# Pooled attention and two dense blocks on one core: VectorE takes over GpSimd's float additions

## The chip, the cores and the metric

One core of one Trainium2 chip runs the whole program. The metric is the device time of one execution in microseconds (us); the figure of a kernel is the median of several executions, and beside it stands one execution that the hardware profiler recorded. The engines are called TensorE (PE, matrix products; PEld is its loading of weights), VectorE (DVE), ScalarE (ACT), GpSimd (POOL) and SyncE (SP, the queue from which all transfers are issued). Each engine works off its own instructions in the order in which they were built.

## The reference

```python
# attention: q, k, v are [8, 8, 576, 64]
k_p = k.reshape(B, H, Sp, 8, D).mean(axis=3)      # Sp = 72
v_p = v.reshape(B, H, Sp, 8, D).mean(axis=3)
scores = (q @ k_p.T) / sqrt(D)
x = softmax(scores) @ v_p                          # -> [4608, 512]
# block 1, weights 512x2048 and 2048x512
h = x @ w_in;  g = where(h >= 1, h, where(h <= -1, 0, (h + 1)**2 / 4))
x2 = g @ w_out
# block 2
h = x2 @ w_in2; r = maximum(h, 0); out = (r * r) @ w_out2
```

The weights arrive as 64-bit words of two 32-bit halves; the kernel makes one float of each pair (`convert_w`). A product in full precision is made of three fast ones, from a rounded part and a remainder of each factor (hi and lo): hi x hi, lo x hi, hi x lo.

## The kernel before

**Order of the program.** The program is written as a list of steps; a scheduler then orders the instructions of each engine when the program is built, by their place in the program and by when it expects their inputs, and inserts the waits. An engine that it expects to be free takes later work that is ready, so pooling runs well ahead of its place in the text. At run time each engine keeps the order given.

**Stages.** The start (about 0 to 45 us) does the attention of the first block of 512 tokens. Then come steps `s`, sixteen (`f`) for each block of 512 tokens: `gemm1` (L656, L666) multiplies x by one column block of the first weights into `ph`; `step_ops` (L670) makes `u` (ScalarE, L689/L690), `g` (VectorE, L699), `gh` (ScalarE, L701) and `gl` (VectorE, L707); `gemm2` (L719, L738) adds `g` times the second weights to four accumulators, two steps later (`LAG`). For each step ScalarE makes `wihi` and `wohi` (L217) and VectorE their remainders `wilo` and `wolo` (L221), from the weights in SBUF. The attention of the next tokens is cut into units that stand between the matmuls (`slots`, L514). From step 28 in the program's text the second block's weights are prepared (`prepare_w2`, L176), and from about 900 us on block 2 runs: its first 512 tokens in the same steps, the rest with seven products in place of eight (L1003, L1012), whose weights are sums and differences of quarters of the weight matrices.

**Weights of block 2.** For each of 16 pairs of weight tiles `prepare_w2` loads both, converts them (`convert_w`, L134: ScalarE, three VectorE operations at L153, L156, L159, one integer addition on GpSimd at L162), forms four sums of quarters (`s1` to `s4`, L196 to L199) and stores all eight quarters as hi and lo with `keep_w2` (L169): ScalarE rounds (L172), an engine given as `lo_on` subtracts (L173), SP stores (L174). Four `keep_w2` calls belong to a pair: VectorE subtracts in two of them and GpSimd in the other two.

**Pooling.** `load_kv` (L267) brings 8 x 64 numbers of 72 groups and two heads as a tile `kv` of 72x2x512; three such buffers exist, and a load waits for the work on the tile that held the buffer. `pool_kv` (L278) halves it by additions: 512, 256, then 128 elements on 72 partitions. Batch 0 has the first two halvings on VectorE for keys and on GpSimd for values (L284), and TensorE does the rest; batches 1 and 2 are pooled by TensorE; batches 3 to 7 (40 tiles) are pooled by GpSimd alone (L297 twice, L298 once). The results `kp` and `vp` go to TensorE's transposes and products.

## Time and profile before

| | |
|---|---|
| median of three runs | 1673.24 us (1672.28 to 1678.28) |
| the profiled execution: its time, its span | 1679.75 us, 1677.7 us |
| TensorE busy (share of the span) | 1640.4 us (98%) |
| VectorE busy | 1237.9 us (74%) |
| ScalarE busy | 885.0 us (53%) |
| GpSimd busy | 327.6 us (20%) |
| mean granted clock of TensorE | 0.989 |

The span runs from the first to the last instruction, the execution's own time is 2.05 us longer. Shares of busy time are averages over stages of different kinds, so the profile is read by stages. A busy TensorE isn't TensorE at its peak: matmuls overlap, and their ends are modelled. Durations of one instruction are in ns in the groups and in us in the timeline; a bracket at the end of a row of the timeline says how long the engine was idle before it and what ended that.

### The profile page before, as it was taken

What the parts mean: (1) busy time and instruction counts of PE and PEld (TensorE: products, weight loads), DVE (VectorE), ACT (ScalarE), POOL (GpSimd) and SP (SyncE); (2) the same over time, 40 slices, a digit from 0 to 9 for tenths busy, and PEclk for the clock granted to TensorE, in tenths of its full rate; (3) what the DMA queues carried; (4) which work ended last, traced back from release to release, by engine and by line L of the source; (5) the groups of instructions that cost most, each with busy time, mean ns of one, the idle gap of its engine ahead of it and who ended that gap; (6) DMA issues with size and microseconds to landing.
All of it is one profiled execution on the core that took longest, in us unless ns stands there. A gap on an engine that the chain in (4) does not pass through costs nothing.

```text
span 1677.7 us, 23589 instructions
## 1 busy us (share of the span) xinstructions
PE 1640.4 (98%) x7952; PEld 1322.4 (79%) x7952; DVE 1237.9 (74%) x1973; ACT 885.0 (53%) x1603; POOL 327.6 (20%) x299
## 2 busy tenths in 40 slices
PE   7899999999999899999999999999999999999998
PEld 6665788888887687878888888888888878887886
DVE  5998578888888888888886452569557856885585
ACT  5655455656566465766666542346435533553353
POOL 3444144542435515231230000000000000000000
PEclk7999999999999999999999999999999999999999
DMA  9475535435354445443543085567686777677675
GB/s 240 134 217 152 144 83 155 148 108 161 112 158 141 118 122 181 123 132 103 192 170 128 7 295 176 170 193 231 191 255 218 207 204 238 213 207 227 194 206 135
DMA packets 276728, 284.72 MB, mean 170 GB/s; under 512 B 151168, under 2 KB 179840, under 8 KB 276608
## 3 DMA queue, kind: packets, MB, share of 16 engines
q1 hardware_dynamic: 276608, 283.21, 56.4%
q8 instruction: 64, 1.05, 0.3%
q14 instruction: 56, 0.46, 0.1%
HBM read 218.10 MB, written 65.01 MB: 169 GB/s over the span
## 4 chain that ended last, share of the span: by engine, by line
PE 84%; DVE 8%; DMA 3%; issue 2%; ACT 1%; POOL 1%; SPq 1%; DVEq 0%; POOLq 0%; ACTq 0%
PE ph L666 22%; PE acc L738 20%; PE dp L1012 10%; PE cp L1003 10%; PE dq L1012 5%; PE cr L1003 5%; PE cq L1003 3%; PE dr L1012 3%; PE px L488 2%; PE pss L372 2%; PE acc L727 2%; DVE wilo L221 1%; DMA w<-w2i 1%; DVE wolo L221 1%; DMA st<-in_moe_w_out_dram 1%
## 5 line engine op out<-in xcount | busy, mean ns | idle before, releaser
L666 PE MATMUL ph<-xhi,wihi 128*128 128x512 f32 x576 | 233.4, 406 | 6.8 <-DVE g L699 5.7
L666 PE MATMUL ph<-xlo,wihi 128*128 128x512 f32 x576 | 226.4, 393 | 0.0
L666 PE MATMUL ph<-xhi,wilo 128*128 128x512 f32 x576 | 226.2, 393 | 0.0
L960 ACT ACTIVATE gh<-g 128x512 fp32r<-128x512 f32 x224 | 139.7, 630 | 151.7 <-DVE g L1029 48.0
L738 PE MATMUL acc<-gh,wohi 128*128 128x512 f32 x512 | 205.9, 402 | 0.0
L738 PE MATMUL acc<-gh,wolo 128*128 128x512 f32 x512 | 200.1, 391 | 1.5 <-DVE wolo L221 1.5
L738 PE MATMUL acc<-gl,wohi 128*128 128x512 f32 x512 | 200.2, 391 | 0.0
L1003 PE MATMUL cp<-x,w 128*128 128x512 f32 x768 | 187.0, 390 | 1.0 <-DMA w<-w2i 0.7
L768 DVE TENSOR_TENSOR gl<-g,gh 128x512 fp32r<-128x512 f32 x224 | 151.3, 687 | 47.6 <-ACT gh L960 46.2
L1003 PEld LDWEIGHTS cp<-x,w 128*128 128x128 f32 x768 | 143.5, 188 | 33.6 <-issue 2.2
L221 DVE TENSOR_TENSOR wilo<-wi,wihi 128x512 fp32r<-128x512 f32 x144 | 123.4, 857 | 58.3 <-ACT wihi L217 57.3
L1012 PE MATMUL dp<-gh,w 128*128 128x512 f32 x512 | 161.5, 389 | 0.0
L707 DVE TENSOR_TENSOR gl<-g,gh 128x512 fp32r<-128x512 f32 x144 | 114.3, 794 | 56.7 <-ACT gh L701 54.1
L666 PEld LDWEIGHTS ph<-xhi,wihi 128*128 128x128 f32 x576 | 109.2, 190 | 35.2 <-DVE g L699 6.1
L217 ACT ACTIVATE wihi<-wi 128x512 fp32r<-128x512 f32 x144 | 89.8, 624 | 81.2 <-PE ph L666 81.0
L666 PEld LDWEIGHTS ph<-xhi,wilo 128*128 128x128 f32 x576 | 109.3, 190 | 23.5
L666 PEld LDWEIGHTS ph<-xlo,wihi 128*128 128x128 f32 x576 | 109.3, 190 | 22.4 <-issue 1.0
L701 ACT ACTIVATE gh<-g 128x512 fp32r<-128x512 f32 x128 | 80.3, 628 | 84.1 <-DVE g L699 83.5
L297 POOL TENSOR_TENSOR kv<-kv 72x512 f32<-72x512 f32 x80 | 93.7, 1173 | 158.4 <-DMA kv<-in_k_dram 81.6
L221 DVE TENSOR_TENSOR wolo<-wo,wohi 128x512 fp32r<-128x512 f32 x128 | 109.2, 853 | 15.3 <-ACT wohi L217 15.1
L1025 ACT ACTIVATE s<-cp 128x512 f32<-128x512 f32 x96 | 57.2, 595 | 118.7 <-PE cp L1003 118.7
L738 PEld LDWEIGHTS acc<-gh,wolo 128*128 128x128 f32 x512 | 96.3, 188 | 21.4 <-DVE wolo L221 2.9
(144 smaller groups left out, 3208.7 us busy)
## 6 DMA issues: line engine op xcount, KB each, us to landing
w<-w2i SPq DMA_DIRECT2D x224, 256.0 KB
w<-w2o SPq DMA_DIRECT2D x224, 256.0 KB
w2i<-cb SPq DMA_DIRECT2D x32, 512.0 KB
w2o<-cb SPq DMA_DIRECT2D x32, 512.0 KB
st<-in_moe_w_out_dram SPq DMA_DIRECT2D x31, 512.0 KB
st<-in_moe_w_in_dram SPq DMA_DIRECT2D x29, 512.0 KB
pd<-pad SPq DMA_DIRECT2D x32, 384.0 KB
z<-pd SPq DMA_DIRECT2D x96, 128.0 KB
```

The source lines that it names most:

```text
L217: nc.scalar.activation(out=hi, in_=src, func=AF.Copy)
L221: eng.tensor_tensor(out=lo, in0=src, in1=hi.bitcast(F32), op=ALU.subtract)
L297: nc.gpsimd.tensor_tensor(out=a[:, :, 0:w], in0=a[:, :, 0:w], in1=a[:, :, w:2 * w], op=ALU.add)
L666: nc.tensor.matmul(out=ph, lhsT=a[:, kk % a.shape[1], :], rhs=c[:, kk, :], start=(i == 0), stop=(i == 3 * KD - 1))
L701: act(out=gh, in_=g, func=AF.Copy)
L707: nc.vector.tensor_tensor(out=gl, in0=g, in1=gh.bitcast(F32), op=ALU.subtract)
L738: nc.tensor.matmul(out=o, lhsT=lhsT, rhs=rhs, start=(f == 0 and x == 0), stop=(f == KF - 1 and x == 2),)
L768: tt(out=out, in0=a, in1=b, op=ALU.subtract)
L960: act(out=hi, in_=a, func=AF.Copy)
L1003: nc.tensor.matmul(out=out[0], lhsT=w[:, a, k, :], rhs=xq[b, i][c][:, k, :], start=(n == 0 and i in (1, 2, 7)), stop=(n == 5), skip_group_ ...
L1012: nc.tensor.matmul(out=out[d], lhsT=w[:, a, d, :], rhs=x[c], start=(g == 0 and n == 0 and i in (1, 2, 7, 4)), stop=(g == NG - 1 and n == 2 ...
L1025: act(out=snaps[key], in_=a, func=AF.Copy)
```

## The change

Every floating-point operation of GpSimd goes to VectorE: the value tiles of batch 0 (8 additions), the pooling of batches 3 to 7 (120 additions), the four sums of quarters of each of 16 pairs (64), and the remainders of these sums (32). GpSimd keeps the 64 integer additions of L162 and some fills of constants.

```diff
-    def keep_w2(kind, g, n, two, lo_on):
+    def keep_w2(kind, g, n, two):
...
-        lo_on.tensor_tensor(out=c[:, :, 1, :], in0=two, in1=c[:, :, 0, :].bitcast(F32), op=ALU.subtract)
+        nc.vector.tensor_tensor(out=c[:, :, 1, :], in0=two, in1=c[:, :, 0, :].bitcast(F32), op=ALU.subtract)
...
-            keep_w2(kind, g, 2 * i, two[i], nc.vector)
+            keep_w2(kind, g, 2 * i, two[i])
...
-        nc.gpsimd.tensor_tensor(out=s1, in0=a21, in1=a22, op=ALU.add)
-        nc.gpsimd.tensor_tensor(out=s2, in0=s1, in1=a11, op=ALU.subtract)
-        nc.gpsimd.tensor_tensor(out=s3, in0=a11, in1=a21, op=ALU.subtract)
-        nc.gpsimd.tensor_tensor(out=s4, in0=a12, in1=s2, op=ALU.subtract)
+        nc.vector.tensor_tensor(out=s1, in0=a21, in1=a22, op=ALU.add)
+        nc.vector.tensor_tensor(out=s2, in0=s1, in1=a11, op=ALU.subtract)
+        nc.vector.tensor_tensor(out=s3, in0=a11, in1=a21, op=ALU.subtract)
+        nc.vector.tensor_tensor(out=s4, in0=a12, in1=s2, op=ALU.subtract)
         yield
-        keep_w2(kind, g, 4, s12, nc.gpsimd)
+        keep_w2(kind, g, 4, s12)
         yield
-        keep_w2(kind, g, 6, s34, nc.gpsimd)
+        keep_w2(kind, g, 6, s34)
...
-                (nc.vector if nm == "k" else nc.gpsimd).tensor_tensor(
-                    out=a[:, :, 0:w], in0=a[:, :, 0:w], in1=a[:, :, w:2 * w], op=ALU.add
-                )
+                nc.vector.tensor_tensor(out=a[:, :, 0:w], in0=a[:, :, 0:w], in1=a[:, :, w:2 * w], op=ALU.add)
...
-            nc.gpsimd.tensor_tensor(out=a[:, :, 0:w], in0=a[:, :, 0:w], in1=a[:, :, w:2 * w], op=ALU.add)
-        nc.gpsimd.tensor_tensor(out=o, in0=a[:, :, 0:D], in1=a[:, :, D:2 * D], op=ALU.add)
+            nc.vector.tensor_tensor(out=a[:, :, 0:w], in0=a[:, :, 0:w], in1=a[:, :, w:2 * w], op=ALU.add)
+        nc.vector.tensor_tensor(out=o, in0=a[:, :, 0:D], in1=a[:, :, D:2 * D], op=ALU.add)
```

The scheduler makes a new order from this. Two places of it follow; lines after L284 are lower by two in the changed kernel. First GpSimd, before, at the first pair of weights of block 2 and the first pooling of batch 3 (`z` is a converted tile, `s` a pair of sums, `cb` a tile to be stored):

```order
L162 TENSOR_TENSOR z<-st,z 128x512 x2
L196 TENSOR_TENSOR s_2712<-z 128x256
L197 TENSOR_TENSOR s_2712<-s_2712,z 128x256
L198 TENSOR_TENSOR z<-z 128x256
L199 TENSOR_TENSOR z<-z,s_2712 128x256
L173 TENSOR_TENSOR cb<-s_2712,cb 128x2x256
L173 TENSOR_TENSOR cb<-z,cb 128x2x256
L162 TENSOR_TENSOR z<-st,z 128x512
L297 TENSOR_TENSOR kv<-kv 72x2x256
L297 TENSOR_TENSOR kv<-kv 72x2x128
L298 TENSOR_TENSOR kp<-kv 72x128
```

GpSimd in the changed kernel, from the last conversions of block 1 to its end:

```order
L162 TENSOR_TENSOR wo_1275<-low_1277,wo_1275 128x512
L162 TENSOR_TENSOR wi_1279<-low_1281,wi_1279 128x512
L162 TENSOR_TENSOR wo_1341<-low_1343,wo_1341 128x512
L162 TENSOR_TENSOR wo_1345<-low_1347,wo_1345 128x512
L162 TENSOR_TENSOR wo_1407<-low_1409,wo_1407 128x512
L162 TENSOR_TENSOR wo_1411<-low_1413,wo_1411 128x512
L162 TENSOR_TENSOR z<-st,z 128x512 x32
```

The integer additions for block 2 now follow each other with nothing between them. The other place is VectorE's order where the first keys of batch 3 are pooled, before (`pn` and `mx` belong to the softmax, `aT` is a turned tile of probabilities):

```order
L699 SCALAR_TENSOR_TENSOR g<-ph,u 128x512
L707 TENSOR_TENSOR gl<-g,gh 128x512
L221 TENSOR_TENSOR wolo<-wo_720,wohi 128x512
L478 STREAM_TRANSPOSE aT<-z 96x1024
L221 TENSOR_TENSOR wilo<-wi_657,wihi 128x512
L390 TENSOR_REDUCE mx<-pss 128x4
L699 SCALAR_TENSOR_TENSOR g<-ph,u 128x512
```

and in the changed kernel:

```order
L697 SCALAR_TENSOR_TENSOR g<-ph,u 128x512
L295 TENSOR_TENSOR kv<-kv 72x2x256
L295 TENSOR_TENSOR kv<-kv 72x2x128
L705 TENSOR_TENSOR gl<-g,gh 128x512
L221 TENSOR_TENSOR wolo<-wo_720,wohi 128x512
L476 STREAM_TRANSPOSE aT<-z 96x1024
L296 TENSOR_TENSOR kp<-kv 72x128
L221 TENSOR_TENSOR wilo<-wi_657,wihi 128x512
L388 TENSOR_REDUCE mx<-pss 128x4
L697 SCALAR_TENSOR_TENSOR g<-ph,u 128x512
```

The three additions of a key tile stand between the operations of a step, the first of them right behind `g` and ahead of `gl`.

## Rows read from the trace of the kernel before

**Rows 1.** Busy time by stages; each engine's us and (instructions), clock, DMA share, GB/s.
```profile
50.00:150.00 100.00, 91.90 (x526) 60.12 (x524) 94.83 (x156) 60.72 (x113) 41.91 (x29) 1.00 0.65 186
150.00:900.00 750.00, 741.13 (x3835) 598.37 (x3835) 611.72 (x974) 454.52 (x842) 269.81 (x248) 1.00 0.46 142
900.00:1050.00 150.00, 150.00 (x664) 124.20 (x663) 70.58 (x108) 65.84 (x112) 0.00 (x0) 1.00 0.41 134
```
**Rows 2.** Busy time in three short stretches (PE, PEld, DVE, ACT, POOL, clock).
```profile
570.00:590.00 20.00, 13.09 (x46) 10.09 (x45) 17.84 (x22) 8.83 (x16) 10.69 (x10) 0.83 0.38 107
650.00:675.00 25.00, 24.19 (x121) 19.63 (x120) 21.38 (x34) 13.35 (x25) 11.44 (x10) 1.00 0.49 163
800.00:825.00 25.00, 24.18 (x121) 19.80 (x120) 20.84 (x39) 14.80 (x27) 2.96 (x2) 1.00 0.44 147
```
**Rows 3.** Timeline from 570 us: start, duration, engine, operation, idle time before and releaser.
```profile
570.43 2.69 DVE L221 TENSOR_TENSOR wolo<-wo,wohi 128x512 fp32r<-128x512 f32 x1
...
572.54 4.64 POOL L297 TENSOR_TENSOR kv<-kv 72x512 f32<-72x512 f32 x4
...
573.18 0.50 PE L738 MATMUL acc<-gh,wolo 128*128 128x512 f32 x1 [1.20 <-DVE wolo L221]
...
576.52 2.42 DVE L221 TENSOR_TENSOR wilo<-wi,wihi 128x512 fp32r<-128x512 f32 x1
...
578.87 2.14 DVE L441 TENSOR_TENSOR pad<-pn,sm 128x256 f32<-128x256 f32 x2
...
581.67 0.80 PE L666 MATMUL ph<-xhi,wihi 128*128 128x512 f32 x1 [5.71 <-DVE g L699]
```
**Rows 4.** Chain that ended last, after that stop: start, us, what.
```profile
581.67 5.49 PE ph L666 x12
...
590.68 2.72 PE ph L666 x12
```
**Rows 5.** Groups of VectorE between 900 and 1050 us, GpSimd idle (busy us, mean ns).
```profile
L707 DVE TENSOR_TENSOR gl<-g,gh 128x512 fp32r<-128x512 f32 x28 | 19.4, 692 | 10.7 <-ACT gh L701 9.1
...
L221 DVE TENSOR_TENSOR wolo<-wo,wohi 128x512 fp32r<-128x512 f32 x13 | 8.9, 686 | 0.0
```
**Rows 6.** Groups of VectorE between 150 and 900 us.
```profile
L221 DVE TENSOR_TENSOR wilo<-wi,wihi 128x512 fp32r<-128x512 f32 x118 | 101.9, 864 | 40.4 <-ACT wihi L217 40.3
L221 DVE TENSOR_TENSOR wolo<-wo,wohi 128x512 fp32r<-128x512 f32 x113 | 97.8, 865 | 13.2 <-ACT wohi L217 13.0
L707 DVE TENSOR_TENSOR gl<-g,gh 128x512 fp32r<-128x512 f32 x115 | 94.2, 820 | 45.8 <-ACT gh L701 45.1
L699 DVE SCALAR_TENSOR_TENSOR g<-ph,u 128x512 f32<-128x512 f32 x115 | 78.3, 681 | 7.9 <-ACT u L690 7.4
L441 DVE TENSOR_TENSOR pad<-pn,sm 128x256 f32<-128x256 f32 x56 | 37.5, 689 | 0.3
```
**Rows 7.** Groups of VectorE over the span: pooling of keys in the start.
```profile
L284 DVE TENSOR_TENSOR kv<-kv 72x512 f32<-72x512 f32 x4 | 2.7, 687 | 6.7 <-DMA kv<-in_k_dram 6.7
...
L284 DVE TENSOR_TENSOR kv<-kv 72x256 f32<-72x256 f32 x4 | 1.7, 420 | 0.1
```
**Rows 8.** Groups of GpSimd over the span: the integer additions for block 2.
```profile
L162 POOL TENSOR_TENSOR z<-st,z 128x512 int32<-128x512 int32 x32 | 50.3, 1573 | 302.6 <-DVE z L159 102.0 <-ACT wohi L217 58.7 <-ACT u L689 45.7
```
**Rows 9.** Timeline of VectorE in the start.
```profile
19.80 0.95 DVE L432 TENSOR_SCALAR sm<-sm 128x8 f32<-128x8 f32 x1
...
24.98 1.23 DVE L432 TENSOR_SCALAR sm<-sm 128x8 f32<-128x8 f32 x1
...
27.58 0.16 DVE L432 TENSOR_SCALAR sm<-sm 128x8 f32<-128x8 f32 x1
...
37.05 0.69 DVE L221 TENSOR_TENSOR wilo<-wi,wihi 128x512 fp32r<-128x512 f32 x1 [4.23 <-ACT wihi L217]
```
**Rows 10.** Waits of GpSimd: us in total, times, longest.
```profile
POOL kv L297 <- DMA kv<-in_k_dram: 81.6, 10, 12.8
POOL kv L297 <- DMA kv<-in_v_dram: 73.7, 7, 14.4
```

## The prediction

> **What bounds the kernel now.** I first read the busy table of the stages [rows 1]. From 150 to 900 us TensorE is busy for 741.13 of 750 us at full granted clock, and in this stretch lie all of the weight sums and of the pooling for batches 3 to 7. VectorE is busy for 611.72 us there (82%), GpSimd for 269.81 us. From 50 to 150 us it is the other way round: VectorE has 94.83 of 100 us, TensorE only 91.90; GpSimd does nothing there but integer additions (29 of them), which the change keeps. From 900 us GpSimd's column is empty. So time can be won only where TensorE stands still between 150 and 900 us, or in the start.
>
> The busy table of three short stretches [rows 2] and the timeline around 570 us [rows 3] show such places. At 570.43 VectorE's remainder `wolo` takes 2.69 us and at 576.52 `wilo` takes 2.42 us, two `pad` products behind them 2.14 us, while GpSimd runs without a pause through pooling and remainders (four additions from 572.54 in 4.64 us). TensorE waits 1.20 us for `wolo`, then 5.71 us for `g`, which stood behind all this in VectorE's queue. The stop costs twice: the granted clock of 570 to 590 us falls to 0.83, and the twelve matmuls of the next step take 5.49 us, those of the step after 2.72 us [rows 4].
>
> Why VectorE is slow there is read from one operation in two stages. With GpSimd idle a remainder of 128x512 takes 0.69 us [rows 5]; between 150 and 900 us the same ones take 0.864, 0.865 and 0.820 us on the mean [rows 6]. The `g` of L699, one input of which is in PSUM, takes 0.681 us in this stretch, as long as any without GpSimd beside it. So it is GpSimd running at the same time that stretches what reads two operands from SBUF.
>
> **The change part by part.** *Added to VectorE after 150 us.* Pooling: 40 pairs of additions on 72x512 and 72x256 elements. On VectorE these shapes stand in the start, with 0.687 and 0.420 us [rows 7]; 40 x 1.107 = 44.3 us. The 40 last additions on 72x128 are not in VectorE's trace; they lie between 0.16 us (a scalar operation on 8 elements, [rows 9]) and 0.420 us (256 elements). I take 0.29 us, since 128 elements lie about halfway: 11.6 us (6.4 to 16.8). The Trainium skill, "VectorE: DVE Perf Modes", section "Side-by-side: where the cycles go for N=2048 bf16", would price this addition at about 0.30 us (128 + 8 + 150 cycles at 0.96 GHz); my estimate from it is 11.9 us, no different sum. Weight sums: 64 on 128x256 at 0.420 us = 26.9 us; remainders: 32 on 128x512 at 0.687 us = 22.0 us. Together 104.8 us (99.6 to 110).
>
> *Taken from VectorE.* What GpSimd costs it now after 150 us: `wilo` 118 x (0.864 - 0.686), `wolo` 113 x (0.865 - 0.686), `gl` 115 x (0.820 - 0.692), `pad` 56 x (0.689 - 0.420) us [rows 5 to 7] = 21.0 + 20.2 + 14.7 + 15.1 = 71 us; smaller groups I leave out. The 31 integer additions that start after 150 us (the first of the 32 for block 2 starts just before) hold 31 x 1.573 = 48.8 of GpSimd's 269.81 us [rows 1, 8], or 18%; I let 82% of the loss go, 58 us (bounds: nothing, or all 71 us). So VectorE gets 104.8 - 58 = 47 us more: 659 of 750 us, 88% (85% to 96%). That isn't full, and TensorE remains the bound of the stretch; on the path this costs 0.
>
> The bounds take in a rule. The Trainium skill, "SBUF — State Buffer", section "Who interferes with whom", says that a VectorE instruction with two SBUF inputs and a GpSimd instruction that reads SBUF exclude each other until the first has finished. The rows above agree (0.865 against 0.686 us, and no stretch where an input is in PSUM). By it each remaining integer addition could hold VectorE for its whole 1.57 us, 49 us in all in place of my 12; VectorE would then be at 93%, and the sum on the path would not move.
>
> *What goes from the path.* With the GpSimd trains the stop at 570 us loses its cause: 1.20 + 5.71 us of waiting [rows 3], and 5.49 - 2.72 = 2.77 us of slow clock [rows 4], together 9.7 us. The two small gaps, 25.00 - 24.19 and 25.00 - 24.18 us [rows 2], stand behind remainders and integer additions as well; I let them go too: 1.6 us. Sum 11.3 us. GpSimd's remaining additions come two to a pair of weight tiles, each behind three VectorE operations, so a train like that at 570 us can't form again. What is late next at such a place is TensorE itself: the matmuls follow each other.
>
> *The start.* Four v tiles are pooled on VectorE in place of GpSimd, between its softmax operations: 4 x 1.107 = 4.4 us more. Against it the operations that now stand beside that pooling shrink: a scalar operation on 128x8 elements takes 0.95 and 1.23 us, the same one 0.16 us elsewhere; 1.9 us back [rows 9]. The rest, 2.5 us, is covered by VectorE's wait of 4.23 us before the first `wilo` at 37.05 us [rows 9]. Cost 0; without that cover 2.5 us, and at best 1 us gained. From 50 to 150 us the integer additions stay as they are, and so does VectorE's load: 0.
>
> *Queues.* No transfer is added or taken away. But a key or value tile's next load, and the 32 stores of summed quarters (`w2i<-cb`, `w2o<-cb`), wait in SP's queue for an operation that was GpSimd's and is now VectorE's. A short VectorE queue answers as soon as GpSimd's did, and nothing reads the stored quarters before 900 us, so I cost it at nothing; if a load comes late, that is case C below. ScalarE no longer waits behind GpSimd's queue for the sums; no credit, since ScalarE is busy for 454.52 of 750 us [rows 1].
>
> **Sum.** 1679.75 us is the profiled execution's own time (span 1677.7 us). Less 11.3 us that is 1668.5 us. The three runs shown lie at 1672.28 to 1678.28 us, median 1673.24, so the profiled one is 6.5 us slower than the median, and the runs differ among themselves by 6 us. I take this as the size of the 570 us stop, which differs from run to run as transfers land earlier or later. Without it the runs should agree at the profiled sum. I forecast 1668.5 us, 0.3% below the median. A difference under 0.5% (8.4 us: below 1664.9 or above 1681.6 us) is about what a measurement of this kernel can't tell from no change.
>
> **Rivals.** *A. The gain is whole in every run.* If the profiled execution is slower for another reason and each run holds the whole 11.3 us, then 1673.24 - 11.3 = 1661.9 us. For it: the start may give another microsecond. Against it: a run at 1672.28 us is hard to read with the same stops as one at 1679.75. Chance 0.27.
>
> *B. Other stops take the place.* VectorE goes from 82% to 88%, and a short wait is harder to make up; one stop of half the old size comes back: 1668.5 + 5 = 1673.5 us. For it: from 50 to 150 us VectorE is just as full with integer additions alone, and TensorE loses 8.1 us in 100 there [rows 1]. Against it: GpSimd has 18% of its work left after 150 us, so what stretches VectorE is rarer than now. Chance 0.20.
>
> *C. Slower: VectorE waits at the head of its queue for a key or value tile.* GpSimd stood 81.6 + 73.7 us before pooling additions, in 17 waits of up to 14.4 us, until a transfer had landed [rows 10]; this cost nothing, since nothing urgent was behind it. Now remainders and `g` are behind it. For it: the place of each addition is fixed when the program is built, whenever the transfer lands in a run. A wait decides from about 5 us on: so much the three stretched pieces of [rows 3] cost VectorE over their usual 0.69, 0.69 and 2 x 0.42 us (2.0 + 1.7 + 1.3), and TensorE lost 6.9 us by it. Two such stops, each 9.7 us, more than eat the gain: 1668.5 + 2 x 9.7 = 1687.9 us. Against it: GpSimd waited because it had nothing else to do; on VectorE every addition stands behind work of its own step. The Trainium skill, "Perfetto Trace Analysis", section "Tensor Engine Instruction (MATMUL, LD_WEIGHTS)", calls VectorE a strict FIFO, and by it nothing could pass a waiting addition. In the timeline [rows 3] `g` indeed came after the `pad` products, although TensorE was waiting for it. Chance 0.13.
>
> That the change doesn't do what it says is excluded: its order leaves GpSimd with 64 integer additions and no other arithmetic.
>
> **How the numbers follow.** Forecast 0.40, A 0.27, B 0.20, C 0.13. Faster by over 0.5%: A, and little of the forecast's edge, 0.29. Slower: C, 0.13. Within: 0.58. The range takes in A with the microsecond of the start, the forecast, B, and the half of C in which a single stop comes with the start's 2.5 us: 1660 to 1681 us.
>
> **What would show it.** Right: between 150 and 900 us VectorE busy for about 659 us, its 128x512 remainders near 0.72 us on the mean and none above 2 us, GpSimd near 49 us, TensorE without a wait of over 2 us, and granted clock 1.00 in each stretch after 150 us. Wrong: a group of waits of VectorE for key or value transfers with a TensorE wait behind it (C); a stop of several microseconds behind `wolo` or `g` elsewhere (B); or a first `ph` step much later than 43 us, which would put the change of time into the start.

## The result, and the profile after

The changed kernel takes 1657.84 us (median of 4 runs, 1657.23 to 1658.98) beside 1672.76 us for the kernel before (4 runs, 1669.71 to 1678.28): ratio 0.9908, 95% interval 0.9881 to 0.9935. It is faster by 0.9%. The forecast of 1668.5 us had the direction right and the size too small; the time lies below the range. The profiled execution of the changed kernel took 1657.23 us (span 1655.5 us), 22.5 us less than the profiled one of the kernel before.

The busy table by stages of the changed kernel (each engine's us and instructions, clock, DMA share, GB/s), to be held against [rows 1]:

```profile
50.00:150.00 100.00, 92.92 (x445) 59.73 (x443) 91.85 (x157) 60.38 (x112) 41.04 (x28) 0.98 0.70 203
150.00:900.00 750.00, 750.00 (x3889) 609.07 (x3888) 631.83 (x1199) 470.92 (x858) 51.15 (x30) 1.00 0.46 140
900.00:1050.00 150.00, 150.00 (x664) 124.22 (x663) 66.35 (x101) 57.66 (x98) 0.00 (x0) 1.00 0.48 156
```

From 150 to 900 us TensorE is busy without a break, at full granted clock. GpSimd fell from 269.81 to 51.15 us. VectorE executes 225 more instructions (1199 for 974) and is busy for only 20 us longer. The groups of VectorE in this stretch show why (as [rows 6]: busy us, mean ns of one):

```profile
L221 DVE TENSOR_TENSOR wilo<-wi,wihi 128x512 fp32r<-128x512 f32 x123 | 92.1, 749 | 63.1 <-ACT wihi L217 61.7 <-PE acc L736 1.0
L221 DVE TENSOR_TENSOR wolo<-wo,wohi 128x512 fp32r<-128x512 f32 x117 | 83.3, 712 | 7.3 <-ACT wohi L217 7.0
L705 DVE TENSOR_TENSOR gl<-g,gh 128x512 fp32r<-128x512 f32 x120 | 81.9, 682 | 18.6 <-ACT gh L699 17.8
...
L295 DVE TENSOR_TENSOR kv<-kv 72x512 f32<-72x512 f32 x40 | 26.9, 678 | 0.0
...
L439 DVE TENSOR_TENSOR pad<-pn,sm 128x256 f32<-128x256 f32 x56 | 23.1, 437 | 0.1
...
L295 DVE TENSOR_TENSOR kv<-kv 72x256 f32<-72x256 f32 x40 | 17.1, 430 | 0.1
...
L296 DVE TENSOR_TENSOR vp<-kv 72x128 f32<-72x128 f32 x20 | 6.7, 337 | 0.1
...
L198 DVE TENSOR_TENSOR z<-z 128x256 f32<-128x256 f32 x16 | 6.6, 411 | 0.1
...
L296 DVE TENSOR_TENSOR kp<-kv 72x128 f32<-72x128 f32 x20 | 5.5, 280 | 0.2
```

The remainders and products fell to 749, 712, 682 and 437 ns, from 864, 865, 820 and 689. The pooling additions (L295, L296) have no idle time in front of them: VectorE did not wait at the head of its queue for a key or value tile.

**Where the 22.5 us came from.** I compared when the same matmul starts in the two profiled executions. The first step of the layer loop starts at 35.55 us instead of 43.03. This lead of 7.5 us is 8.0 at 175 us, still 8.0 at 500 us, and 8.3 at 545 us. It is 18.5 at about 600 us, after the place of the old stop; 20.8 at 850 us; 21.4 at 1035 us, where the steps with seven products begin; 22.2 at the end. So 8 us came from the start, 13.4 us from the loop, and 1 us from the rest. This divides the difference of two single executions; the medians differ by 14.9 us.

In the start, TensorE's clock is what differs. First the timeline of TensorE in the kernel before (start, duration, operation, idle time before and releaser), then the same of the changed kernel:

```profile
22.32 1.07 PE L453 MATMUL pt<-ident,pad 128*72 128x128 f32 x8 [1.14 <-DVE pad L436]
...
25.20 1.90 PE L453 MATMUL pt<-ident,pad 128*72 128x128 f32 x8 [1.38 <-DVE pad L436]
...
32.84 1.98 PE L488 MATMUL px<-aT,vp 72*64 72x128 f32 x16
...
43.03 1.22 PE L666 MATMUL ph<-xhi,wihi 128*128 128x512 f32 x2 [1.09 <-ACT xhi L500]
```

```profile
23.04 0.60 PE L451 MATMUL pt<-ident,pad 128*72 128x128 f32 x4 [1.29 <-DVE sm L430]
...
31.62 1.99 PE L486 MATMUL px<-aT,vp 72*64 72x128 f32 x32
...
35.55 1.31 PE L664 MATMUL ph<-xhi,wihi 128*128 128x512 f32 x2 [1.95 <-DVE wi L156]
```

The second wait for `pad` before is one for a scaling that VectorE makes while GpSimd pools a value tile; after the change the same scaling takes 0.75 us. First the two rows of before, then the one of after:

```profile
23.72 3.27 POOL L284 TENSOR_TENSOR kv<-kv 72x256 f32<-72x256 f32 x3
23.78 1.27 DVE L436 TENSOR_TENSOR pad<-pad,sm 128x576 f32<-128x576 f32 x1
```

```profile
22.15 0.75 DVE L434 TENSOR_TENSOR pad<-pad,sm 128x576 f32<-128x576 f32 x1
```

Sixteen `px` matmuls took 1.98 us before; thirty-two take 1.99 us now. The busy tables by 4 us give the granted clock (TensorE's us and instructions, clock, DMA share, GB/s), before and then after:

```profile
24.00:28.00 4.00, 2.80 (x14) 0.55 1.05 342
28.00:32.00 4.00, 4.00 (x25) 0.50 1.01 289
...
40.00:44.00 4.00, 2.91 (x20) 0.50 0.18 64
44.00:48.00 4.00, 4.00 (x11) 0.50 0.03 6
```

```profile
24.00:28.00 4.00, 3.23 (x27) 1.00 1.04 356
28.00:32.00 4.00, 4.00 (x52) 1.00 0.95 260
...
36.00:40.00 4.00, 4.00 (x12) 0.62 0.93 314
```

Before, TensorE idled 1.14 and 1.38 us for the scalings of `pad`, and after the second idle time it ran at 0.50 (1.2 GHz) until 48 us. In the changed kernel, whose TensorE also has a wait of 1.29 us before 23.04 us, the clock stays at 1.00 (2.4 GHz) until 32 us. Why one wait is followed by the slow clock and the other is not can't be read from these two executions; the experiments come back to it.

### The profile page after: what moved, and what is told of

Its sections match the earlier page's. It is cut to its first block, busy times and chain, and to the rows that moved or that the text cites. A ratio compares the mean times of both kernels' runs of the same rounds, so it can differ in the third digit from the quotient of the medians.

```text
span 1655.5 us, 23521 instructions
## 1 busy us (share of the span) xinstructions
PE 1626.6 (98%) x7952; PEld 1315.0 (79%) x7952; DVE 1248.3 (75%) x2197; ACT 890.9 (54%) x1603; POOL 103.1 (6%) x75
## 4 chain that ended last, share of the span: by engine, by line
PE 92%; DVE 3%; DMA 2%; issue 1%; SPq 1%; ACT 0%; DVEq 0%; ACTq 0%
PE ph L664 26%; PE acc L736 24%; PE dp L1010 11%; PE cp L1001 10%; PE dq L1010 5%; PE cr L1001 5%; PE dr L1010 3%; PE cq L1001 2%; PE pss L370 2%; PE px L486 2%; PE acc L725 2%; PE pv L327 1%; DMA w<-w2i 1%; DMA q<-in_q_dram 0%; DMA kv<-in_v_dram 0%
## 5 line engine op out<-in xcount | busy, mean ns | idle before, releaser
L766 DVE TENSOR_TENSOR gl<-g,gh 128x512 fp32r<-128x512 f32 x224 | 150.8, 685 | 47.6 <-ACT gh L958 46.1
L221 DVE TENSOR_TENSOR wilo<-wi,wihi 128x512 fp32r<-128x512 f32 x144 | 109.2, 758 | 75.4 <-ACT wihi L217 71.3
L705 DVE TENSOR_TENSOR gl<-g,gh 128x512 fp32r<-128x512 f32 x144 | 98.5, 684 | 26.0 <-ACT gh L699 23.4
L736 PEld LDWEIGHTS acc<-gl,wohi 128*128 128x128 f32 x512 | 96.1, 188 | 21.3
L1010 PEld LDWEIGHTS dp<-gh,w 128*128 128x128 f32 x512 | 96.1, 188 | 19.9
L736 PEld LDWEIGHTS acc<-gh,wohi 128*128 128x128 f32 x512 | 96.2, 188 | 19.4 <-issue 0.8
```

What stands on the lines that cost most here:

```text
L221: eng.tensor_tensor(out=lo, in0=src, in1=hi.bitcast(F32), op=ALU.subtract)
L705: nc.vector.tensor_tensor(out=gl, in0=g, in1=gh.bitcast(F32), op=ALU.subtract)
L736: nc.tensor.matmul(out=o, lhsT=lhsT, rhs=rhs, start=(f == 0 and x == 0), stop=(f == KF - 1 and x == 2),)
L766: tt(out=out, in0=a, in1=b, op=ALU.subtract)
L1010: nc.tensor.matmul(out=out[d], lhsT=w[:, a, d, :], rhs=x[c], start=(g == 0 and n == 0 and i in (1, 2, 7, 4)), stop=(g == NG - 1 and n == 2 ...
```

## The experiments

Three questions: which part of the change gives which gain; whether GpSimd slows VectorE by what it reads, or by being late itself; and whether the start's gain is the clock. The kernel before was run again beside each group of kernels; its medians there were 1673.54 to 1677.08 us, and each ratio is against the runs of its own group. The changed kernel was not run again: where a kernel is held against its 1657.84 us, the runs are of different groups. The best runs of the kernel before in these groups lie within 1.7 us of each other (1668.64 to 1670.28 us).

### One part at a time

**Start only** (the kernel before, with the first batch's value tiles pooled on VectorE):

```diff
-                (nc.vector if nm == "k" else nc.gpsimd).tensor_tensor(
-                    out=a[:, :, 0:w], in0=a[:, :, 0:w], in1=a[:, :, w:2 * w], op=ALU.add
-                )
+                nc.vector.tensor_tensor(out=a[:, :, 0:w], in0=a[:, :, 0:w], in1=a[:, :, w:2 * w], op=ALU.add)
```

> The kernel before with one part of the change: VectorE pools the value tiles of batch 0 (8 additions), all else as before. Theory 1 (the change gained in two places, the start and the stop near 570 us, and the start's gain is this part): the softmax operations of the start no longer stand beside GpSimd, TensorE's short gaps before 26 us get shorter, its granted clock stays near 1.00 from 24 to 48 us (before 0.50 to 0.55), the first ph matmul comes near 36 us (before 43.0), and the time falls by about 8 us to 1665 us; the stop near 570 us may come or not as before. Theory 2 (the start's gain is a chance of the clock, or comes from the order of later instructions): the first ph stays near 43 us, time 1672.8 within 3 us.

1675.0 us (10 runs, 1672.95 to 1679.04), ratio 0.9987 (0.9967 to 1.0008). In its profile the first step starts at 35.4 us and the clock is 1.00 from 24 to 36 us: the start's gain is there. Its row of the loop:

```profile
150.00:900.00 750.00, 738.99 (x3817) 596.03 (x3816) 602.66 (x970) 456.45 (x843) 259.54 (x242) 1.00 0.46 139
```

TensorE loses 11 us there, most of it in seven stops of 0.85 to 2.5 us. The part works in its own place, as Theory 1 said, and no gain is left at the end: the 1665 us of Theory 1 did not come.

**Pooling of batches 3 to 7 only** (the kernel before, with these lines):

```diff
-            nc.gpsimd.tensor_tensor(out=a[:, :, 0:w], in0=a[:, :, 0:w], in1=a[:, :, w:2 * w], op=ALU.add)
-        nc.gpsimd.tensor_tensor(out=o, in0=a[:, :, 0:D], in1=a[:, :, D:2 * D], op=ALU.add)
+            nc.vector.tensor_tensor(out=a[:, :, 0:w], in0=a[:, :, 0:w], in1=a[:, :, w:2 * w], op=ALU.add)
+        nc.vector.tensor_tensor(out=o, in0=a[:, :, 0:D], in1=a[:, :, D:2 * D], op=ALU.add)
```

> The kernel before with the pooling of batches 3 to 7 on VectorE (120 additions), all else as before. Theory 1: the start stays as before (first ph near 43 us); pooling was about half of GpSimd's float work after 150 us and of the train at 570 us, so the stop there goes for the most part: 1663 to 1668 us, remainders of 128x512 on VectorE near 0.77 us on the mean between 150 and 900 us. Theory 2 (pooling at the head of VectorE's queue waits for transfers): waits of VectorE for kv transfers of over 5 us in all, with TensorE waits behind them, time 1673 us or more.

1665.89 us (10 runs, 1662.07 to 1671.91), ratio 0.9946 (0.9920 to 0.9971). The time is that of Theory 1, and so are the remainders, 0.75 to 0.78 us on the mean; VectorE waits 0.2 us in all for key or value tiles, so Theory 2 is out. The start is not as Theory 1 had it. GpSimd pools the value tiles as before, TensorE waits 1.38 us for `pad` as before, and yet the clock stays at 1.00 and the first step starts at 36.43 us:

```profile
24.31 1.04 PE L453 MATMUL pt<-ident,pad 128*72 128x128 f32 x8 [1.38 <-DVE pad L436]
...
36.43 0.89 PE L666 MATMUL ph<-xhi,wihi 128*128 128x512 f32 x2 [0.69 <-ACT xhi L500]
```

```profile
28.00:32.00 4.00, 4.00 (x49) 1.00 1.08 298
```

Up to 36 us TensorE, VectorE, ScalarE and GpSimd execute the instructions of the kernel before in its order. With the same work in the same order the first step thus starts at 43.03 us in one execution and at 36.43 us in the other; the changed kernel's is at 35.55. The two executions part at 16.5 us, where four `pss` matmuls still take 1.17 us in the kernel before and 0.66 us here; the wait for the first `pad` is then 1.14 us there and 0.28 us here. By these executions 6.6 of the 7.5 us of the start are the clock, and 0.9 us are operands that come earlier.

**Weight sums and remainders only** (the kernel before, with the four sums and the two remainders of sums on VectorE):

```diff
-        nc.gpsimd.tensor_tensor(out=s1, in0=a21, in1=a22, op=ALU.add)
+        nc.vector.tensor_tensor(out=s1, in0=a21, in1=a22, op=ALU.add)
...
-        keep_w2(kind, g, 4, s12, nc.gpsimd)
+        keep_w2(kind, g, 4, s12, nc.vector)
```

> The kernel before with the sums of weight quarters and their remainders on VectorE (96 operations), all else as before. Theory 1: the start stays as before (first ph near 43 us); the stop near 570 us goes for the most part, as GpSimd's additions there come from both kinds of work, 1663 to 1668 us. Rival: the stop is due to pooling alone (it is the longer train, 4.64 us for four additions); then it stays and the time is 1670 to 1675 us.

1666.8 us (10 runs, 1660.24 to 1669.72), ratio 0.9937 (0.9913 to 0.9961). The rival (pooling alone makes the stop) is out. In its profile the first step starts at 40.73 us and the clock is 0.50 from 28 to 44 us. TensorE's loss between 150 and 900 us in the two kernels' profiles, 3.8 and 0.7 us, first of pooling only, then of weights only:

```profile
150.00:900.00 750.00, 746.16 (x3866) 604.61 (x3865) 624.83 (x1100) 464.03 (x856) 158.74 (x127) 1.00 0.46 140
```

```profile
150.00:900.00 750.00, 749.30 (x3888) 606.15 (x3887) 628.83 (x1084) 467.11 (x857) 167.85 (x152) 1.00 0.46 142
```

Before it was 8.9 us [rows 1]. Either half alone removes most of the stops: 5.0 and 8.2 us of 8.9. The gains do not add. I read this as a stop needing a train of GpSimd instructions long enough to use up VectorE's slack, so that halving the trains is nearly enough; no run varies the length of a train by itself. The medians of both kernels also mix runs that keep the clock in the start with runs that don't (1662.1 to 1664.1 us at 0.996 or more and 1671.0 to 1671.9 at 0.991 or less, with only the pooling moved).

**All but the start** (the changed kernel, with the value tiles of the first batch back on GpSimd):

```diff
-                nc.vector.tensor_tensor(out=a[:, :, 0:w], in0=a[:, :, 0:w], in1=a[:, :, w:2 * w], op=ALU.add)
+                (nc.vector if nm == "k" else nc.gpsimd).tensor_tensor(
+                    out=a[:, :, 0:w], in0=a[:, :, 0:w], in1=a[:, :, w:2 * w], op=ALU.add
+                )
```

> The changed kernel with the value tiles of batch 0 back on GpSimd. Theory 1: the start is that of before (first ph near 43 us, clock near 0.5 from 24 to 48 us), the rest that of the changed kernel, with no TensorE wait over 1 us between 150 and 900 us: 1657.8 + 8 = 1666 us. Theory 2 (the start's gain has nothing to do with who pools these tiles): first ph near 36 us, 1658 us.

1665.49 us (10 runs, 1658.55 to 1668.77), ratio 0.9938 (0.9914 to 0.9963): Theory 1. The first step starts at 40.75 us. The wait for the second `pad`, and the busy table of start and loop:

```profile
23.55 1.04 PE L453 MATMUL pt<-ident,pad 128*72 128x128 f32 x8 [1.38 <-DVE pad L436]
```

```profile
24.00:28.00 4.00, 3.65 (x25) 2.70 (x23) 3.87 (x11) 3.13 (x6) 1.44 (x3) 0.66 1.08 366
28.00:32.00 4.00, 4.00 (x29) 2.85 (x29) 3.09 (x4) 1.94 (x4) 1.31 (x1) 0.50 0.96 248
150.00:900.00 750.00, 750.00 (x3890) 606.58 (x3889) 636.60 (x1206) 470.76 (x859) 53.43 (x32) 1.00 0.47 142
```

The loop is whole and the start is slow. Of its ten runs, two took 1658.55 and 1658.58 us at a mean granted clock of 0.997 and 0.996 over the run; the other eight took 1663.5 to 1668.8 us at 0.993 or less. I read the two as runs that kept the clock in the start; only one run, of the eight, was profiled. Then such a run equals the changed kernel. Up to 36 us this kernel, too, executes the kernel before's instructions in their order, so its profile can be held against that of "pooling only": in both TensorE waits 1.38 us for the second `pad`, 0.2 to 0.3 us for the first, and 0.35 us for GpSimd's value tile behind it. Here the clock falls to 0.50, there it stays at 1.00. The waits alone thus don't settle it; what does is not in these rows. The kernel before has the same spread: of its 17 runs beside the last group of kernels, ten at 0.992 or more took 1669.5 to 1675.3 us, and seven at 0.991 or less took 1676.2 to 1682.0.

### What GpSimd does to VectorE in the loop

**Echo in the loop.** The changed kernel, with GpSimd repeating on dead data what was taken from it; the orders of TensorE, ScalarE and VectorE stay those of the changed kernel but for one or two neighbouring instructions:

```diff
         nc.vector.tensor_tensor(out=o, in0=a[:, :, 0:D], in1=a[:, :, D:2 * D], op=ALU.add)
+        for w in (4 * D, 2 * D, D):
+            nc.gpsimd.tensor_tensor(out=a[:, :, 4 * D:4 * D + w], in0=a[:, :, 4 * D:4 * D + w], in1=a[:, :, 0:w], op=ALU.add)
...
+        for _ in range(4):
+            nc.gpsimd.tensor_tensor(out=two[1][:, 0, :], in0=two[1][:, 0, :], in1=two[1][:, 1, :], op=ALU.subtract)
...
+        if echo:
+            nc.gpsimd.tensor_tensor(out=two, in0=two, in1=c[:, :, 0, :].bitcast(F32), op=ALU.subtract)
```

> The changed kernel, with its VectorE, TensorE and ScalarE orders kept as they are; GpSimd repeats on dead data what the change took from it in the loop (three additions for each key or value tile from the fourth batch on, four subtractions for each set of sums, two remainders). Theory 1 (sharing: what the change gained in the loop is that GpSimd no longer slows VectorE's instructions): VectorE's busy time from 150 to 900 us rises from 631.8 to 680 to 700 us, weight remainders from a mean of 758 to about 840 ns, and TensorE stops of 4 to 12 us in sum come back between 150 and 900 us: 1662 to 1670 us. Theory 2 (place in the order: what was gained is that the pooled tiles and sums no longer wait for GpSimd): VectorE's instructions are slowed as well, but TensorE does not stop, 1656 to 1660 us.

1688.41 us (5 runs, 1687.48 to 1691.98), ratio 1.0078 (1.0051 to 1.0105): 30.6 us slower than the changed kernel and slower than the kernel before. Its busy row, and then groups of its VectorE:

```profile
150.00:900.00 750.00, 728.82 (x3741) 584.67 (x3740) 677.23 (x1165) 439.61 (x820) 336.81 (x245) 0.99 0.45 136
```

```profile
L225 DVE TENSOR_TENSOR wilo<-wi,wihi 128x512 fp32r<-128x512 f32 x116 | 93.3, 805 | 19.4 <-ACT wihi L221 19.4
...
L299 DVE TENSOR_TENSOR kv<-kv 72x512 f32<-72x512 f32 x40 | 33.1, 832 | 0.0
...
L299 DVE TENSOR_TENSOR kv<-kv 72x256 f32<-72x256 f32 x40 | 25.7, 646 | 0.1
```

The pooling that VectorE took over is itself stretched, 678 to 832 ns and 430 to 646 ns. TensorE loses 21 us in this stretch; the waits of TensorE for `g` (9.2 us in six) and for the turned `aT` (5.6 us in three) hold most of it. The loss is larger than Theory 1 said, probably because VectorE now carries the moved work and the stretching together, and because the echo holds GpSimd longer (336.81 us) than its work before (269.81). That VectorE waits for tiles which GpSimd frees late is out: it has no idle time before the pooling additions.

**Memsets in the loop.** The same kernel, each echoed instruction replaced by two memsets of the same region:

```diff
...
-            nc.gpsimd.tensor_tensor(out=a[:, :, 4 * D:4 * D + w], in0=a[:, :, 4 * D:4 * D + w], in1=a[:, :, 0:w], op=ALU.add)
+            for _ in range(2):
+                nc.gpsimd.memset(a[:, :, 4 * D:4 * D + w], 0.0)
```

> The kernel of the echo in the loop with each repeated two-operand instruction of GpSimd replaced by two memsets of the same dead region: GpSimd's queue, the hold on the tiles and the integer additions queued behind are much as in that run, but GpSimd reads nothing. Theory 1 (sharing: VectorE is slowed by GpSimd's two-operand reads, and nothing else of GpSimd's work matters): VectorE's busy time from 150 to 900 us stays near the changed kernel's 631.8, below 645, no TensorE stop over 1 us there, 1656 to 1661 us. Theory 2 (occupancy: the tiles are freed late and the integer additions come late because GpSimd's queue is long): at least half of that run's loss of 30.6 us remains, 1670 us or more.

1657.08 us (4 runs, 1655.09 to 1658.41), ratio 0.9882 (0.9855 to 0.9908): as fast as the changed kernel.

```profile
150.00:900.00 750.00, 750.00 (x3889) 609.07 (x3888) 631.37 (x1196) 470.69 (x857) 198.83 (x460) 1.00 0.46 139
```

GpSimd is busy for 198.83 us, more than in the kernel with only the pooling moved (158.74), and VectorE's 631.37 us is that of the changed kernel. So at this length of queue neither GpSimd's busy time nor the tiles that it holds cost anything; its two-operand instructions do. The Trainium skill, "SBUF — State Buffer", section "Who interferes with whom", says that a VectorE instruction with two SBUF inputs contends with a GpSimd instruction that reads SBUF, not with one that only writes it. The two runs agree: 1688.41 us with reads, 1657.08 without.

One thing the memsets do not bring back. ScalarE rounds the converted weights (`cb`, L172) and waits for GpSimd's integer additions; first with the echo, then with the memsets (us in total, times, longest):

```profile
ACT cb L172 <- POOL z L162: 73.0, 29, 6.5
```

```profile
ACT cb L172 <- POOL z L162: 32.4, 26, 2.9
```

In the changed kernel it is 32.9 us. At 333 us of the echo ScalarE has just stood still for 5.02 us for such an addition, and TensorE for 2.32 us for `g`. So part of the 30.6 us may come by way of ScalarE, because GpSimd's own two-operand instructions take longer and hold up the integer additions; the runs don't divide the loss between this and the stretching of VectorE.

### The same in the start

**Echo in the start.** The changed kernel, with GpSimd repeating the eight additions of the first batch's value tiles; the orders of TensorE, VectorE and ScalarE are the changed kernel's:

```diff
+            if nm == "v":
+                for w in (4 * D, 2 * D):
+                    nc.gpsimd.tensor_tensor(out=a[:, :, 4 * D:4 * D + w], in0=a[:, :, 4 * D:4 * D + w], in1=a[:, :, 0:w], op=ALU.add)
```

> The changed kernel, with the orders of VectorE, TensorE and ScalarE kept; GpSimd repeats on dead data the two additions for each of the four value tiles of the first batch, which the change took from it. Theory 1 (sharing): the scalings of pad and pn between 20 and 26 us are slowed again, TensorE's gaps there grow, and its granted clock falls to about 0.5 before the first step of the layer loop in a good part of the runs: median 1660 to 1668 us with a spread of 6 us or more, as in the kernel that left only this part on GpSimd (1658.6 to 1668.8). Theory 2 (order): TensorE and VectorE do the same in the same order as in the changed kernel, so the first step stays at 35 to 36 us and the runs within 2 us of 1657.8.

1664.81 us (6 runs, 1663.43 to 1665.85), ratio 0.9931 (0.9908 to 0.9955): 7 us slower than the changed kernel. The median is Theory 1's; the spread of 2.4 us is not: every run lies above 1663 us. Nor are the instructions those of Theory 1: the two scalings of `pad` take 0.75 us as in the changed kernel, since the echo starts at 23.87 us, after both. It is five of VectorE's own additions that take 5.50 us in place of 2.29; TensorE waits 0.83 and 2.11 us for them, and there the clock falls.

**Memsets in the start** (two memsets in place of each addition):

> The kernel of the echo in the start with each of GpSimd's eight repeated additions replaced by two memsets of the same dead region; all other orders as in the changed kernel. Theory 1 (sharing by two-operand reads): VectorE's value additions and the scalings after them take as long as in the changed kernel (five additions in 2.3 us, not 5.5), the first step of the layer loop starts at 35 to 36 us at a granted clock of 1.00, and the time is 1656 to 1660 us. Theory 2 (GpSimd's queue: the integer additions of the first weights come late behind the repeated work): first step after 37 us and 1661 us or more.

1656.91 us (5 runs, 1655.71 to 1664.59), ratio 0.9906 (0.9879 to 0.9933). Three runs took 1655.7 to 1656.9 us; two took 1663.3 and 1664.6, at a mean clock of 0.994. Either the memsets bring back some of the chance, or the four runs of the changed kernel were too few to meet it. VectorE's value and key additions in the start (duration in ns: least, median, most), first with the echo, then with the memsets:

```profile
L284 DVE TENSOR_TENSOR kv<-kv x8: 410/806/1753, 18.4 to 30.1; 72x512 f32<-72x512 f32 x4, 72x256 f32<-72x256 f32 x4
```

```profile
L284 DVE TENSOR_TENSOR kv<-kv x8: 414/526/681, 17.5 to 26.0; 72x512 f32<-72x512 f32 x4, 72x256 f32<-72x256 f32 x4
```

With the echo the first step starts at 43.2 us and the clock is 0.50 from 32 to 40 us; with the memsets it starts at 35.1 us.

### Is it the clock?

**Fill without the start part**, and **fill in the kernel before**: TensorE multiplies the identity by itself while it would idle for `pad`, into a bank that the next transposes overwrite. The first is made from the kernel "all but the start", the second from the kernel before; the edit is the same:

```diff
+        for i in range({(0, 0): 8, (1, 0): 10}.get((t, g), 0)):
+            nc.tensor.matmul(out=pt[:, i % 4, :], lhsT=ident, rhs=ident, start=True, stop=True)
         for i in range(4):
```

> The changed kernel with the first batch's value tiles left on GpSimd (as in the run before of this part alone), and 18 more matmuls of identity by identity in TensorE's two gaps between 20 and 26 us, into banks that the next step overwrites. Theory 1 (clock: late operands open two gaps of 1.1 to 1.4 us, after which the granted clock falls to 0.5 in some runs and the following 100 small matmuls take twice as long): granted clock 0.95 or more from 16 to 36 us, first step of the layer loop at 35 to 38 us, median 1657 to 1661 us and a spread under 5 us. Theory 2 (lateness: the pooled values themselves come too late, whatever the clock): first step at 39 to 42 us in the profile, median 1663 to 1668 us and a spread of 8 us or more.

1660.52 us (6 runs, 1658.65 to 1663.44), ratio 0.9907 (0.9882 to 0.9931); 5 us less than without the fill (1665.49, measured beside other runs), and a spread of 4.8 us in place of 10.2. The clock is 1.00 from 16 to 32 us and 0.99 to 36; the first step starts at 38.2 us, not 40.8. That is still 2.7 us later than in the changed kernel: TensorE waits 2.08 us for a copy of `aT`, and the clock falls after that; from 150 to 900 us it is 1.4 us later, where "all but the start" is 9.8 us later. By the medians the fill brings back 5.0 of the 7.7 us between "all but the start" and the changed kernel. It also reorders VectorE's work after it, so these shares are rough; that most of the start's loss is the clock agrees with the 6.6 of 7.5 us found above. The fill shows as well that the clock falls for TensorE's idle time: with the waits filled none of six runs has a mean clock under 0.995, without the fill eight of ten are at 0.993 or less.

> The kernel before, with 18 matmuls of identity by identity in TensorE's two gaps between 20 and 26 us and nothing else; GpSimd keeps all its float work. Theory 1 (clock in the start, then the loop's own stops): granted clock 0.95 or more from 16 to 32 us in the profile, the first step of the layer loop at 37 to 39 us in place of 43.0, no run of 1680 us or more as the kernel before has them, but the loop stops of the kernel before remain: 150 to 900 us with 738 to 743 us of TensorE, median 1669 to 1676 us. Theory 2 (the start's 8 us reach the end of the program by themselves): median 1662 to 1668 us. Theory 3 (the clock was not the cause): first step at 41 to 44 us and runs spread from 1669 to 1683 us as before.

1675.91 us (12 runs, 1672.25 to 1679.33), ratio 1.0007 (0.9993 to 1.0021). Its busy rows in the start, and in the loop:

```profile
24.00:28.00 4.00, 4.00 (x41) 1.00 1.06 359
28.00:32.00 4.00, 3.49 (x41) 1.00 1.00 259
```

```profile
150.00:900.00 750.00, 740.88 (x3829) 598.29 (x3828) 599.03 (x974) 459.45 (x847) 260.27 (x244) 1.00 0.46 140
```

The first step starts at 37.6 us, and no run reaches 1680 us; of the 17 of the kernel before beside it one did. But TensorE still loses 9.1 us in the loop, with GpSimd at 260.27 us, and the median gains nothing. A mended start is worth little in this kernel while the loop has its stops: the runs of the kernel before that keep their clock are near this median already, and the best of them (1669.5 us) are below it. By their times these must lose less in the loop than the two kernels with a mended start; why was not seen, since none of them was profiled.

### A further attempt

**Fill ahead of the first step** in the changed kernel, in the gap of 1.95 us before 35.55 us, with 14 matmuls and then with 8 (the second keeps the order of every engine):

```diff
+        for _ in range(14 if s == 0 else 0):
+            nc.tensor.matmul(out=ph[:, 0:P], lhsT=ident, rhs=ident, start=True, stop=True)
```

> The changed kernel with 14 matmuls of identity by identity in the gap of 1.95 us that TensorE has ahead of the first step of the layer loop, into the bank that this step overwrites. Theory 1 (clock): the granted clock from 36 to 40 us goes from 0.62 to 0.95 or more, the first 12 matmuls of the step take about 2.7 us in place of 4.6, and the time is 1 to 2 us under the changed kernel's 1657.8: 1655.5 to 1657 us. Theory 2 (the step's operands set the pace there, so a faster clock waits for the next weight): no gain, 1657 to 1660 us.

1663.9 us (6 runs, 1662.55 to 1667.05), ratio 0.9930 (0.9903 to 0.9957), worse than the changed kernel. The clock from 36 to 40 us is 1.00 and the first twelve matmuls of the step take 2.7 us, not 4.5; but the fill runs 1.3 us past the gap, the program's order differs after it, and TensorE idles 5.45 us for `pn` at 58 us in place of 2.71.

> The changed kernel with 8 matmuls of identity by identity in TensorE's gap of 1.95 us ahead of the first step of the layer loop; unlike the run with 14, the orders of all engines stay those of the changed kernel. Theory 1 (clock): the granted clock from 36 to 40 us rises from 0.62 to 0.95 or more, the first 12 matmuls of the step take about 2.7 us in place of 4.6, and the time is 1 to 2 us under the changed kernel's, 1655.5 to 1657 us; the run with 14 was slower only because its order differs after 50 us. Theory 2 (the operands set the pace there, so a faster clock waits for the next one): 1657 to 1659 us. Theory 3 (the remaining gap of about 1 us lowers the clock all the same): clock 0.6 at 36 to 40 us and 1657 to 1659 us.

1659.34 us (6 runs, 1655.52 to 1659.98), ratio 0.9890 (0.9866 to 0.9915). TensorE's busy rows of this kernel:

```profile
36.00:40.00 4.00, 3.98 (x21) 1.00 1.09 316
...
52.00:56.00 4.00, 1.60 (x4) 1.00 0.64 189
56.00:60.00 4.00, 2.60 (x8) 0.74 0.91 270
```

The clock at 36 to 40 us is 1.00 as planned, and the wait for `pn` at 57 us grows from 2.71 to 3.81 us. There is no gain, as in Theory 2. I read it as VectorE's conversion of the first weights setting the pace up to 60 us, so that a faster TensorE waits there; this was not tested by itself. No kernel tried is measurably faster than the changed one.

## Why the prediction was wrong

**What failed: the start, "Cost 0; without that cover 2.5 us, and at best 1 us gained".** I added up VectorE's instructions there and asked whether 2.5 us more would be covered. I did not look at the granted clock of the first 50 us. In the profiled execution it was 0.50 from 28 to 48 us, after two waits of TensorE for scalings of `pad`, the second of which ran beside GpSimd's pooling. The value was 8.0 us in this execution, where I had put 0. "Pooling only" has the same start with the clock kept and its first step at 36.43 us, so the clock is 6.6 us of it; the fill shows that the clock falls for TensorE's waits. The echo (43.2 us for the first step) against the memsets (35.1 us) shows that GpSimd's reads can open such waits, there on other instructions. Whether the clock falls differs from one execution to the next.

**What failed with it: the run spread as "the size of the 570 us stop".** The profiled execution was 6.5 us over the median and had a mean granted clock of 0.989. Of the 70 runs of the kernel before beside the experiments, 29 are at 0.991 or less, and all but one of them (1672.87 us) lie above 1676 us; the 18 at 0.995 or more lie between 1668.6 and 1673.5 us. And leaving only the start on GpSimd is enough to bring such a spread into a kernel whose loop has no stop. So the start's clock accounts for a large part of the spread. I subtracted 11.3 us from an execution that also held 8 us of slow start; 1679.75 - 11.3 - 8.0 = 1660.5 us would have come out, near the 1657.84 measured. For the median this sum is no account: there the start alone gained nothing (1675.0 us), though the change without it takes 1665.49 and with it 1657.84.

**The loop's sum, 11.3 us: right in mechanism, short in size.** Measured 13.4 us. The 570 us stop was put at 9.7 us; the lead grows there by 18.5 - 8.3 = 10.2 us. The two small gaps were put at 1.6; from 600 to 850 us the lead grows by 2.3. Another 0.3 us come before 545 us and the last 0.6 after 850 us. One of the small gaps went although its cause stayed: the one at 817 us stood behind a remainder of 1.80 us beside an integer addition, and the changed kernel keeps these additions and has remainders of up to 1.81 us. Either the forecast was lucky there, or VectorE's queue had more room; the runs don't show which.

**Added and taken off: half right.** The added operations cost what was forecast: 678 and 430 ns for the pairs (0.687 and 0.420 forecast), 280 and 337 ns for the last addition (0.29), about 415 ns for a sum. But VectorE came to 631.83 us, not 659. The four groups lost 123 x 0.115 + 117 x 0.153 + 120 x 0.138 + 56 x 0.252 = 62.7 us, by their means above and in [rows 6], where I had let 58 us go (so 13 us were to stay, not the 12 that I wrote). The rest is in two places. The durations of all groups together rise by 35 us (671 to 706), but records of back-to-back instructions overlap, and busy time rises by only 20. And the smaller groups that I left out shrink too, operations with one input among them: `z` of L153 from 522 to 416 ns, `sm` of L432 from 253 to 161. So the stretching is not confined to instructions that read two operands from SBUF, as I had put it; [rows 9] show that already.

**A term put at nothing: ScalarE behind GpSimd.** ScalarE's waits for GpSimd's results fell from 93.7 us (150 to 900 us, before) to 32.9 us. I gave this no credit; no run shows what it is worth, and the echo shows only that it can be part of a loss.

**Its tests.** Wrong: VectorE at 631.83 us, not 659. Right: remainders of 0.75 and 0.71 us on the mean (0.72 forecast), none above 2 us (the longest is 1.81), GpSimd 51.15 us, no TensorE wait between 150 and 900 us, clock 1.00 there. The test on the start was set for a first step later than 43 us; it came earlier.

**Rivals.** A is nearest: the median less the whole gain of the loop, 1661.9 us. I read the missing 4 us as the loop's other 2 us and a start that no longer slows some runs; no run divides them. B, other stops in their place, did not come in the changed kernel; it did come in the kernel with only the start moved, whose loop kept its trains. C did not come: no pooling addition after 150 us waited for a tile.

## What to carry to other kernels

Read the granted clock of the first tens of microseconds as closely as the loop's: in some executions, waits of little over 1 us on operations that another engine stretches were followed by half the clock for up to 24 us, and the matmuls behind them took twice as long. Such a loss comes in some runs and not in others, so hold a profiled execution's time and mean clock against those of the other runs before taking a difference from it. A two-operand float operation moved from GpSimd to VectorE can cost less than its own duration, since it also ends the stretching of VectorE's other two-operand work; here 105 us of added operations raised VectorE's busy time by 20 us (35 us by the durations of its groups). Work of GpSimd that only writes cost nothing here and could stay.

## What was not expected of the hardware

GpSimd was busy for 199 of 750 us, with memsets and the integer additions, at no cost, while 337 us of two-operand instructions cost 30.6 us. The stretching goes both ways: in the kernel with the echo an addition of 72x512 elements took GpSimd 2118 ns on the mean beside VectorE's own of the same shape (832 ns); in the kernel before it took 1427 ns. And TensorE's clock after gaps of the same length was not the same: a wait of 1.29 us before 23.04 us left it at 1.00 in the changed kernel, one of 1.38 us before 25.20 us was followed by 0.50 in the kernel before, and with the same instructions in the same order a wait of 1.38 us was followed by 0.50 in "all but the start" and by 1.00 in "pooling only". The mean clock of "all but the start" over a run was 0.989 in one run and 0.997 in another. The Trainium skill, "TensorE: Matmul & The Clock Gate", section "Part 1: The HAM clock gate (the "warmup" mystery)", tells of differences between runs of one kernel in how many matmuls run at the slow clock at its beginning, puts the cost of that at under 1% of a typical kernel's span and advises against fitting a model to one count of them. The size agrees with the rows here: 8 us, 0.5% of the span. But it was a third of the difference between the two profiled executions.
